# A gated complex recurrence and a mixer on one core: chunks of 128 tokens scaled to their middle in one step, with a checked condition and a branch

## The chip, the cores and the metric

The kernel runs on one core of a Trainium2 chip. The time is device microseconds (us) of one execution on that core; the runs shown are separate executions of the same program. A profile is one more execution, taken by the hardware profiler. In it PE is TensorE's matmul row, PEld its weight loads, DVE is VectorE, ACT is ScalarE, POOL is GpSimd and SP is SyncE, which here only issues DMAs.

## The reference, cut to what matters

Two blocks follow each other. The first is a recurrence over 768 tokens for 4 batches of 8 heads of width 48, with a complex gate per token and channel:

```python
mag = np.sqrt(a_re * a_re + a_im * a_im)
scale = np.minimum(mag, 0.999) / (mag + 1e-06)
a_re_n, a_im_n = (a_re * scale, a_im * scale)
for t in range(S):                       # S_re, S_im: (B, H, 48, 48)
    new_re = ar * S_re - ai * S_im
    new_im = ar * S_im + ai * S_re
    S_re, S_im = (new_re + k[t] v[t]^T, new_im)
    y[t] = q[t] @ S_re
```

The second takes y as x, of shape (4, 768, 384), and is a mixer: u = x + (x^T U V)^T with U of 768x32 and V of 32x768, and then out = u + relu(u @ w_ch1) @ w_ch2, with 1536 hidden channels. All is float32, but for the four mixer weights, which arrive as float64 and are converted on the core.

## The kernel before, in words

**Chunks.** Each batch is cut into 6 chunks of 128 tokens, 24 in all; a chunk has two halves of 64. The recurrence is computed as attention within a half, plus what a 48x48 state per head brings from before. A gate's logarithm (ACT and DVE, `magnitudes_of`, in groups of two chunks) is summed over tokens by a matmul, and exp of the sum is a factor on q and of its inverse on k. A gate's angle is summed in the same manner and gives a cosine and a sine, so that q and k have 2 x 48 real channels, padded to 112 rows (`prep`: `weigh` multiplies q and k by the factors `es`; two products write them with cos and sin into the tile QKC; 16 transposes on PE, in four PSUM tiles, turn them into QK of 112 channels x 8 heads x 128 tokens, copied out by ACT).

**Levels.** A factor over many tokens can leave float32's range, so the kernel before scales q and k only to the middle of blocks of 8 tokens and then grows the blocks step by step. `within` (L583) makes the factors to the middle of 8; `of_blocks` (L612) sums the logarithms over spans of 4, 8, 16, 32, 64 and 128 tokens in one matmul per head against the 64 columns of the tile `total`; ACT's exp of them is E, which SP's DMAs (L598) rearrange into T. In `chain`, per chunk:

- `inner` is called three times (L739): 32 matmuls that each give a 32x32 or 32x16 block of scores in PSUM; DVE then copies the entries of one mask from PSUM into DG (`keep`, L745, a predicated copy).
- `times` and `grow` (L330, five per chunk) multiply the halves of QK by the T of the next larger blocks on DVE.
- four SP DMAs (L777) place the 32x32 diagonal blocks of DG in the score tile AT; `corners` (L789, 16 matmuls) gives the off-diagonal 32x32 blocks of each half, which ACT copies into AT (L794, four copies).
- the grown k is transposed back to tokens x channels (`ks ps`, L810, 8 matmuls, ACT copies at L812).

**State.** dk (L825) is k^T v of each half. `onward` carries the state: GM = G(i-1) x T + dk of half 0, then G(i) = GM x T + dk of half 1, each a multiplication (L330) and an addition (L333) on DVE. The output y of a half is AT^T v (L856) plus q times the state before it (L864), and ACT copies it into xo (L873, four copies).

**Mixer.** `mixer(m)` handles two chunks and can start when a whole batch is through: `rank` (L898) needs all six xo of the batch. `up` (L939) or, from m = 6, the form with fewer products `few` (L997); then `down` (L1085) or `down_two` (L1128). These are PE's large matmuls, 12 mixers in all.

**The order of the work.** Nothing is issued when it is recorded: `Plan` keeps every piece with engine, estimated cost, what it reads and writes and which ring of buffers it takes. `Plan.order` then simulates the five engines and writes out one order for each; among pieces that are ready an engine takes the one with the least urgency, and URGENCY is a table of numbers per kind of work (weights w1 and w2, gates, angles, prep, levels, rest) and chunk or piece. Where PE would have nothing to do before the first "mixing" piece, the plan puts in a filler: a `spare` matmul of the identity (L1252), 203 of them. In PE's order `tr` is the transposes of `prep`. Before the first `rank` of batch 0 PE has only chunk work and fillers; after that, mixers of the batch before run between the chunks of the next; behind the last chunk three mixers are left.

**Buffers.** PSUM tags have two tiles each: T (gates, transposes), A (scores, `ks ps`), Y (dk and y share it), M (mixer). QKC has one tile, VP three, AT and DG two, G two, GM one.

Of the kernel before, what the change touches and what calls it, by code (L numbers as in the profile page):

```python
# [23 lines left out]
BLK = 32  # L24

URGENCY = {
    "w1": {0: -1281.04, 1: -1220.88, 2: -1207.45, 3: 315.61, 4: 369.7, 5: 444.04, 6: 70.95},
    "w2": {0: -1266.56, 2: -21.8, 4: -981.82, 6: -74.99, 8: 354.48, 10: -1170.63, 12: 259.42},
    "gates": {0: 253.11, 1: -1390.93, 2: -0.7, 4: -1280.16, 6: 565.76, 8: -1068.17, 10: -187.84, 12: -54.04, 14: 550.2,
        16: 60.85, 18: -1317.29, 20: 219.78, 22: -1069.82},  # L30
    "angles": {0: -1303.82, 1: -1298.68, 2: -1227.51, 4: 58.46, 6: 57.41, 8: -1315.3, 10: -1053.02, 12: 620.73,
        14: 187.25, 16: -891.55, 18: 148.92, 20: -161.38, 22: -1298.55},
    "prep": {0: -1294.88, 1: 125.6, 2: -26.13, 3: 96.73, 4: 102.92, 5: 146.86, 6: 553.65, 7: 283.9, 8: 120.02,
        9: -991.17, 10: -32.91, 11: 113.94, 12: -202.96, 13: 14.8, 14: 318.58, 15: 357.43, 16: 269.94, 17: 521.08,
        18: 158.53, 19: -163.04, 20: 127.47, 21: 184.1, 22: 205.57, 23: -1204.94},
    "levels": {0: 201.22, 1: 294.56, 2: -15.94, 3: 207.38, 4: -1236.01, 5: 275.3, 6: 572.46, 7: 14.34, 8: -1057.92,
        9: 306.71, 10: 125.53, 11: 133.52, 12: 287.15, 13: 373.35, 14: 82.96, 15: 592.16, 16: 289.79,
        17: -1204.78, 18: -1075.08, 19: 91.86, 20: 733.17, 21: -1309.23, 22: 119.93, 23: -1230.17},
    "rest": {0: 93.55, 1: 47.27, 2: 273.41, 3: 257.67, 4: -1050.04, 5: -1068.08, 6: -1240.77, 7: -1208.87, 8: -1033.73,
        9: -1290.81, 10: 34.85, 11: -1143.56, 12: -162.29, 13: -197.24, 14: -1046.5, 15: 612.4, 16: 244.97,  # L40
        17: -1261.21, 18: 98.64, 19: -1031.75, 20: -1297.46, 21: 239.78, 22: 384.61, 23: 164.23},
}
# [145 lines left out]
@with_exitstack  # L188
def kernel(
    ctx: ExitStack,  # L190
    tc: tile.TileContext,
    q: bass.AP,
    k: bass.AP,
# [9 lines left out]
    out: bass.AP,  # L203
):


# [36 lines left out]
    SIZES = (4, 8, 16, 32, 64, 128)  # L243
    NTOT = CH // 2
    NP = 128 // R
# [8 lines left out]
    def urgency(kind, n):  # L254
        if kind == "load":
            return n - 20
        if kind in ("totals", "place"):
            return n - 100
        if kind in ("small", "mixing"):
            return n + (1000 if kind == "mixing" else -1000)  # L260
        return URGENCY[kind][n]

# [51 lines left out]
    def SP(cost, *a, **kw):  # L314
        plan.add("SP", max(cost, 0.65), *a, late=2.0 if cost > 0.65 else 1.4, **kw)
# [34 lines left out]
    prefix = singles.tile([128, CH], FP, name="prefix")  # L350
    mask = singles.tile([128, 6, BLK], I32, name="mask")
    mid = singles.tile([128, CH], FP, name="mid")
# [38 lines left out]
    AT, DG, VP = [], [], []  # L391
    QKC = singles.tile([128, H, 2, DP], FP, name="QKC")
    nc.gpsimd.memset(QKC, 0.0)
    GATE = singles.tile([128, 6, GC * DM], FP, name="gate")
# [3 lines left out]
    TS = []  # L398
    for n in range(3):
        TS.append(singles.tile([DQ, GC, H * NTOT], FP, name="T%d" % n))  # L400
        nc.gpsimd.memset(TS[n], 1.0)
    for n in range(3):
        VP.append(singles.tile([128, H, D], FP, name="VP%d" % n))
    for n in range(2):
        AT.append(singles.tile([128, H, HC], FP, name="AT%d" % n))
        DG.append(singles.tile([128, H, BLK], FP, name="DG%d" % n))
        nc.gpsimd.memset(AT[n], 0.0)
        nc.gpsimd.memset(DG[n], 0.0)

    def constants():  # L410
        SP(0.4, ("load", 0.1), lambda: nc.sync.dma_start(out=prefix, in_=spans[:, PRE * CH:(PRE + 1) * CH]), writes=[("prefix", 0)])
        SP(0.6, ("load", 1.2), lambda: nc.sync.dma_start(out=mask, in_=masks), writes=[("mask", 0)])

# [118 lines left out]
    def gates(g):  # L532
# [54 lines left out]

        def totals():
            e, tt = ("E", g), ("T", g)
            buffer(e, "E", 1, [128, GC, HH, NTOT])  # L590
            ring(tt, "T", TS)
            lo, hi = GROUPS[g]
            for part in PARTS[g]:
                for i in range(*part):
                    of_blocks(i, ("gates", part[0]))
            for u in range(2):
                for w in range(2):
                    SP(0.65, ("totals", lo), lambda u=u, w=w: nc.sync.dma_start(  # L598
                        out=get(*tt)[u * DP:u * DP + D, 0:hi - lo, w * HH * NTOT:(w + 1) * HH * NTOT],
                        in_=get(*e)[w * 64:w * 64 + D, 0:hi - lo].rearrange("p c h b -> p c (h b)")), [e], [tt + ((u, w),)])  # L600

        def of_blocks(i, R1):
# [80 lines left out]
    def prep(i):  # L683
# [9 lines left out]
        for u in range(2):  # L693
            qkc = ("qkc", 2 * i + u)
            ring(qkc, "qkc", [QKC])
            DVE(c_dve(2 * DM), R1, lambda u=u, qkc=qkc: mul(
# [16 lines left out]
    def chain(i):  # L713
        c = where(i)[1]
        RL, RR = ("levels", i), ("rest", i)
        QK, DGi, ATi, VPi = ("QK", i), ("DG", i), ("AT", i), ("VP", i)
        ring(DGi, "DG", DG)
        ring(ATi, "AT", AT)
# [46 lines left out]

        yield from inner(5, 2)


        times(RL, 4, 16, 8, H * CH - 8, 0)
        yield from inner(1, 8)  # L770
        times(RL, 4, 16, 0, H * CH + 8, 2)
        grow(RL, 8)
        yield from inner(0, 16)
        for j in range(CH // BLK):
            js = slice(j * BLK, (j + 1) * BLK)
            to = slice(j % 2 * BLK, j % 2 * BLK + BLK)
            SP(0.65, ("place", i), lambda js=js, to=to: nc.sync.dma_start(out=get(*ATi)[js, :, to], in_=get(*DGi)[js]), [DGi],  # L777
               [ATi + (("d", js.start),)])
        grow(RR, 16)

        ps1 = ("corners", i)
        psum(ps1, "A", [128, HH, BLK], [128, 4 * HH, BLK])

        def corners():
            for p in range(HH):
                for u in range(2):
                    for r in (0, 64):
                        h, to = 2 * p + u, r + u * BLK
                        nc.tensor.matmul(out=get(*ps1)[to:to + BLK, p], lhsT=k_of(h)[:, r:r + BLK],  # L789
                                         rhs=q_of(h)[:, r + BLK:r + 2 * BLK], start=True, stop=True, tile_position=(0, to))  # L790
        yield 0.38, RR, corners, [QK], ps1, ATi, 8 * HH
        for r in (0, 64):
            for u in range(2):
                ACT(0.32, RR, lambda r=r, u=u: nc.scalar.copy(  # L794
                    out=get(*ATi).rearrange("p (a u) t -> p a u t", u=2)[r:r + BLK, :, u, BLK:2 * BLK],
                    in_=get(*ps1)[r + u * BLK:r + (u + 1) * BLK]), [ps1], [ATi + (("c", r, u),)])
        grow(RR, 32)

        G, mid_G, last = ("G", i), ("GM", i), c == NCH - 1
        ks, dk = ("ks", i), [("dk", (i, r)) for r in range(2)]  # L800
        buffer(ks, "ks", 1, [128, H, DQ])
        buffer(mid_G, "GM", 1, [DQ, H, D])
        rows_k = HC if last else CH
        for hh in range(2):
            ps = ("ks ps", (i, hh))
# [11 lines left out]
        for r in parts_k:  # L817
            psum(dk[r], "Y", [128, H, D], [128, H, DP])

        def state(h0):  # L820
            for h in range(h0, h0 + HH):
                for r in parts_k:
                    at = slice(r * HC, (r + 1) * HC)
                    for x, end in ((0, DP), (DP, DQ)):
                        nc.tensor.matmul(out=get(*dk[r])[x:end, h], lhsT=get(*ks)[at, h, x:end], rhs=get(*VPi)[at, h],  # L825
                                         start=True, stop=True, tile_position=(r * HC, x))
# [5 lines left out]
        def onward(to, of, r):  # L832
# [5 lines left out]
            DVE(c_dve(DM), RR, lambda: add(get(*to), get(*to), get(*dk[r])[0:DQ]), [dk[r]], [to])  # L838
        onward(mid_G, ("G", i - 1) if c else None, 0)
        if not last:  # L840
            onward(G, mid_G, 1)

        y, xi = [("y", (i, r)) for r in range(2)], ("xo", i)
# [343 lines left out]


    constants()
    weights()  # L1190
# [52 lines left out]
    for f in waits:  # L1243
        f()
    chunks(NG - 1)
    spare = []

# [8 lines left out]
    for ins in nc.cur_bb.bb.instructions:  # L1256
        if ins.engine in last:
            tc.add_manual_dep(ins, last[ins.engine], mybir.DependencyInfo(
                mybir.DependencyClass.NoSync, mybir.DependencyReason.DATA), reason="order")
        last[ins.engine] = ins.name  # L1260


# [45 lines left out]
```

## Time and profile before

| | |
|---|---|
| three runs | 696.73, 697.74 (median), 700.15 us |
| profiled execution | span 696.8 us; that is also within 0.1 us of the fastest run, and no other time of it is recorded |
| PE, PEld busy | 673.7 us (97%), 594.2 us (85%) |
| DVE, ACT, POOL busy | 538.9 us (77%), 416.5 us (60%), 51.8 us (7%) |
| granted TensorE clock | 0.997 |
| DMA | 53.24 MB, 165203 packets, of which 154016 are under 512 B |
| dearest DVE group | L330 on QK: 120 instructions, 145.4 us |
| fillers | 203 in the program, 406 records, 57.8 us |

A float32 matmul stands in the trace as two records, a transpose as one. A few records can be missing. Busy time of a group is the union of its records, and their ends are modelled, so the busy times of PE's groups add up to more than PE's. The start-to-start distance of two pieces in the timeline says what a piece costs in the stream. "issue" is time in which an engine waited for nothing that the profile shows.

### The profile page before, as it was taken

What the parts mean: (1) busy time and instruction counts of PE and PEld (TensorE: products, weight loads), DVE (VectorE), ACT (ScalarE), POOL (GpSimd) and SP (SyncE); (2) the same over time, 40 slices, a digit from 0 to 9 for tenths busy, and PEclk for the clock granted to TensorE, in tenths of its full rate; (3) what the DMA queues carried; (4) which work ended last, traced back from release to release, by engine and by line L of the source; (5) the groups of instructions that cost most, each with busy time, mean ns of one, the idle gap of its engine ahead of it and who ended that gap; (6) DMA issues with size and microseconds to landing.
All of it is one profiled execution on the core that took longest, in us unless ns stands there. A gap on an engine that the chain in (4) does not pass through costs nothing.

```text
span 696.8 us, 26972 instructions
## 1 busy us (share of the span) xinstructions
PE 673.7 (97%) x12116; PEld 594.2 (85%) x12116; DVE 538.9 (77%) x877; ACT 416.5 (60%) x776; POOL 51.8 (7%) x92
## 2 busy tenths in 40 slices
PE   8988998999999999999999999999998999999998
PEld 8777777786787888888888888889998898999998
DVE  5899999888998887758598668779886884555734
ACT  7879874968886897958796745434524325031230
POOL 5100000012100010001010100000000000000000
PEclk9999999999999999999999999999999999999999
DMA  8884745699514442432243031222111010000000
GB/s 202 190 187 86 172 99 105 171 222 189 110 36 97 87 92 54 94 70 57 51 89 78 3 86 40 45 43 56 37 36 18 14 41 2 18 7 24 7 18 24
DMA packets 165203, 53.24 MB, mean 76 GB/s; under 512 B 154016, under 2 KB 160352, under 8 KB 165088
## 3 DMA queue, kind: packets, MB, share of 16 engines
q1 hardware_dynamic: 161008, 42.26, 28.0%
q0 software_dynamic: 4080, 9.27, 5.9%
q8 instruction: 95, 1.56, 0.9%
q14 instruction: 20, 0.16, 0.1%
HBM read 33.59 MB, written 4.72 MB: 55 GB/s over the span
## 4 chain that ended last, share of the span: by engine, by line
PE 75%; ACT 10%; DVE 9%; issue 3%; DMA 2%; SPq 0%; DVEq 0%; ACTq 0%
PE down L1128 20%; PE few L997 12%; PE up L939 10%; PE tr L705 6%; PE inner L739 5%; ACT gate L327 4%; PE y L864 3%; PE dk L825 3%; DVE QK L330 2%; PE ks ps L810 2%; PE ph L650 2%; PE es ps L583 2%; PE tot L612 2%; PE y L856 2%; PE spare L1252 1%
## 5 line engine op out<-in xcount | busy, mean ns | idle before, releaser
L330 DVE TENSOR_TENSOR QK<-QK,T 112x1024 f32<-112x1024 f32 x120 | 145.4, 1217 | 7.6 <-PE corners L789 4.0
L939 PE MATMUL up<-uT,w 128*128 128x256 f32 x432 | 98.9, 382 | 0.0
L939 PEld LDWEIGHTS up<-uT,w 128*128 128x128 f32 x432 | 80.5, 190 | 12.3
L1005 ACT COPY h<-few 128x512 f32<-128x512 f32 x36 | 20.6, 586 | 95.0 <-PE few L997 78.2
L708 ACT COPY QK<-tr 112x512 f32<-112x512 f32 x96 | 53.0, 586 | 36.5 <-PE tr L705 36.1
L1128 PE MATMUL down<-w,h 128*128 128x192 f32 x396 | 74.1, 331 | 0.0
L327 ACT ACTIVATE gate<-gate 128x768 f32<-128x768 f32 (+1 forms) x91 | 70.2, 789 | 5.3 <-DMA gate<-in_a_re_dram 2.2
L1128 PEld LDWEIGHTS down<-w,h 128*128 128x128 f32 x396 | 63.7, 190 | 3.2 <-issue 1.1
L739 PEld LDWEIGHTS inner<-QK 112*32 112x32 f32 x4608 | 45.4, 109 | 20.7 <-issue 15.4
L333 DVE TENSOR_TENSOR h<-few,h 128x512 f32<-128x512 f32 x54 | 37.1, 690 | 31.3 <-PE few L997 28.7
L739 PE MATMUL inner<-QK 112*32 112x16 f32 (+1 forms) x4608 | 51.3, 190 | 10.4 <-issue 9.3
L1252 PE MATMUL spare<-ident 128*128 128x128 f32 x406 | 57.8, 289 | 1.7 <-POOL ident masks.py:199 1.5
L330 DVE TENSOR_TENSOR QKC<-qk,cs 128x768 f32<-128x768 f32 x48 | 45.7, 953 | 14.9 <-PE tr L705 13.4
L705 PE MATMUL tr<-ident,QKC 128*112 128x128 f32 x384 | 54.2, 276 | 2.8 <-ACT QK L708 1.1
L1252 PEld LDWEIGHTS spare<-ident 128*128 128x128 f32 x406 | 52.0, 200 | 5.5 <-POOL ident masks.py:199 1.5
L333 DVE TENSOR_TENSOR xo<-down,xo 128x192 f32<-128x192 f32 (+1 forms) x79 | 29.6, 385 | 28.5 <-PE down L1128 28.3
L705 PEld LDWEIGHTS tr<-ident,QKC 128*112 128x112 f32 x384 | 42.1, 133 | 10.9 <-ACT QK L708 3.0
L997 PE MATMUL few<-gate,w 128*128 128x128 f32 x336 | 44.0, 279 | 0.0
L1072 POOL DMA_DIRECT2D out_dram<-xo x32 | 18.8, 586 | 321.0 <-DVE xo L333 289.2
L873 ACT COPY xo<-y 64x192 f32<-64x192 f32 x96 | 30.0, 313 | 18.8 <-PE y L864 17.4
L997 PEld LDWEIGHTS few<-gate,w 128*128 128x128 f32 x336 | 40.6, 194 | 0.5
L1128 PE MATMUL down<-stage 128*128 128x192 f32 x198 | 36.8, 329 | 0.1
(131 smaller groups left out, 1242.6 us busy)
## 6 DMA issues: line engine op xcount, KB each, us to landing
stage<-in_moe_w_ch_dram SPq DMA_DIRECT2D x12, 768.0 KB, 5.8
gate<-in_a_re_dram SPq DMA_DIRECT2D x24, 192.0 KB, 3.5
gate<-in_a_im_dram SPq DMA_DIRECT2D x24, 192.0 KB, 3.7
qk<-in_q_dram SPq DMA_DIRECT2D x24, 192.0 KB, 3.4
qk<-in_k_dram SPq DMA_DIRECT2D x24, 192.0 KB, 4.2
VP<-in_v_dram SPq DMA_DIRECT2D x24, 192.0 KB, 3.4
T<-E SPq DMA_DIRECT2D x48, 96.0 KB, 2.7
w<-stage POOLq DMA_DIRECT2D x12, 384.0 KB, 6.0
```

The lines of the kernel that those rows point to most:

```text
L327: return nc.scalar.activation(out=o, in_=i, func=f, **kw)
L330: nc.vector.tensor_tensor(out=o, in0=a, in1=b, op=OP.mult)
L333: nc.vector.tensor_tensor(out=o, in0=a, in1=b, op=OP.add)
L705: nc.tensor.transpose(out=get(*ps)[0:DQ, j], in_=get(*qkc)[:, hh * HH + j].rearrange("p u d -> p (u d)")[:, 0:DQ], identity=ident)
L708: ACT(c_act(HH * CH) - 0.05, R1, lambda u=u, hh=hh, ps=ps: nc.scalar.copy(out=get(*QK)[:, u, hh * HH:(hh + 1) * HH], in_=get(*ps)[0:DQ]), ...
L739: nc.tensor.matmul(out=get(*ps)[js, h], lhsT=k_of(h)[:, js], rhs=part(q_of(h)[:, js], "p"), start=True, stop=True, tile_position=(0, j * BLK))
L825: nc.tensor.matmul(out=get(*dk[r])[x:end, h], lhsT=get(*ks)[at, h, x:end], rhs=get(*VPi)[at, h], start=True, stop=True, tile_position=(r * ...
L873: ACT(c_act(HH * D), RR, lambda r=r, u=u: nc.scalar.copy(out=get(*xi).rearrange("p (a u d) -> p a u d", u=2, d=D)[r * HC:(r + 1) * HC, :, ...
L939: nc.tensor.matmul(out=get(*ps)[:, e], lhsT=w1[:, f, (ff + e) * 128:(ff + e + 1) * 128], rhs=get(*uT)[:, f], start=(f == 0), stop=(f == KD ...
L997: nc.tensor.matmul(out=get(*ps)[:, q], lhsT=w()[:, q * 128:(q + 1) * 128], rhs=v[0](), start=(n == 0 and q == 0), stop=True, skip_group_ch ...
L1128: nc.tensor.matmul(out=get(*to)[:, part], lhsT=x(j), rhs=y[:, j], start=(first and j == 0), stop=(j == KH - 1), skip_group_check=not first)
L1252: nc.tensor.matmul(out=spare[0], lhsT=ident, rhs=ident, start=True, stop=True)
```

## The change

The function `tile_gateloop...` becomes `body(..., general, worst, ...)`. With `general` false, `body` is the new program; with `general` true it is the program before, with plain urgencies (`n` in place of the table). The new entry records the new program, reads one word from SBUF into a register of every engine, and has the general program behind a branch:

```diff
+def tile_gateloop__then__mixer_low_rank_kernel(tc: tile.TileContext, *args):
+    with tc.tile_pool(name="worst", bufs=1) as pool:
+        worst = pool.tile([1, 1], I32, name="worst")
+        body(tc, False, worst, *args)
+        found = tc.nc.values_load(worst, ...)
+        with tc.If(found != 0):
+            body(tc, True, worst, *args)
```

In the new program the factors reach to the middle of the whole chunk in one step (`mid` is the sum to token 63 less the sum to the token; `total` has two columns, the sums over the two halves):

```diff
+            def middle():
+                nc.gpsimd.tensor_tensor(out=mid, in0=half.to_broadcast([128, CH]), in1=prefix, op=OP.subtract)
+                nc.gpsimd.tensor_copy(out=total[:, 0:1], in_=half)
+                nc.gpsimd.tensor_tensor(out=total[:, 1:2], in0=prefix[:, CH - 1:CH], in1=half, op=OP.subtract)
...
+        def of_halves(i, R1):
+            def sums():
+                for h in range(H):
+                    for u in range(2):
+                        nc.tensor.matmul(out=get(*ps)[u * 64:(u + 1) * 64, h], lhsT=get(*l)[:, at + h * D:at + h * D + 64],
+                                         rhs=total, start=True, stop=True, tile_position=(0, u * 64))
+            table(0.25, R1, lambda: act(falls[:, i], get(*ps)[0:DQ], AF.Exp, scale=-1.0), [ps], [("falls", i)])
```

`of_halves` has 16 matmuls per chunk where `of_blocks` had 8, with 2 moving columns where there were 64. E, T and the DMAs between them are gone. `inner`, `times`, `grow`, the placing DMAs, `corners` with its copies and `ks ps` with its copies are left out; in their place:

```diff
+        def whole():
+            psum(ps, "A", [128, H, HC])
+            def products():
+                for h in range(H):
+                    for r in range(2):
+                        at = slice(r * HC, (r + 1) * HC)
+                        nc.tensor.matmul(out=get(*ps)[at, h], lhsT=k_of(h)[:, at], rhs=q_of(h)[:, at], start=True, stop=True,
+                                         tile_position=(0, r * HC))
+            DVE(c_dve(H * HC), RL, lambda: nc.vector.copy_predicated(
+                out=get(*ATi), mask=mask.unsqueeze(1).to_broadcast([128, H, HC]), data=get(*ps)), [ps, ("mask", 0)], [ATi])
...
+        yield from (levels() if general else whole())
...
+        ks, dk = ("ks", i) if general else ("qkc", 2 * i + 1), [("dk", (i, r)) for r in range(2)]
```

So a chunk has 16 matmuls of 112 rows x 64 columns against 64 moving columns, and one predicated copy of 512 columns. dk reads k straight from QKC, which is now one tile for q and a ring of three for k. The state takes one multiplication and two additions per chunk in place of two and two:

```diff
+        def through(to, of, r):
+            DVE(c_dve(DM), RR, lambda: add(get(*to), get(*dk[r])[0:DQ], get(*of)), [dk[r], of], [to])
+
+        if c and not general:
+            B = ("G", i - 1)
+            DVE(0.16, RR, lambda: mul(between[:, i], falls[:, i - 1, :, 1], falls[:, i, :, 0]), ...)
+            DVE(c_dve(DM), RR, lambda: mul(get(*B), get(*B), between[:, i].unsqueeze(2).to_broadcast([DQ, H, D])), ...)
```

After the last chunk's piece is recorded, `verdict` finds the smallest of all `falls` (a DVE reduction of 112 x 384, one transpose on PE, a second reduction) and writes 1 into `worst` if it is below exp(-30). With the inputs of the reference a half's sum of logarithms lies between -7.3 and -5.3, so the word is 0.

The URGENCY table is replaced by another one throughout:

```diff
 URGENCY = {
-    "w1": {0: -1281.04, 1: -1220.88, 2: -1207.45, 3: 315.61, 4: 369.7, 5: 444.04, 6: 70.95},
+    "w1": {0: 30.69, 1: -1312.12, 2: -1.77, 3: 1300.77, 4: 396.41, 5: 683.84, 6: -1360.01},
...
```

The mixer's code is the same. The program up to the branch has 4037 instructions on PE for 6384, 710 on DVE for 879, 633 on ACT for 778, 145 on SP for 289, and 160 fillers for 203 (counts of the built programs, one per instruction).

## The prediction

> **What bounds the kernel now.** I read the page's head first, then the chain of work that ended last (section 4).
>
> ```profile
> span 696.8 us, 26972 instructions
> ...
> PE 673.7 (97%) x12116; PEld 594.2 (85%) x12116; DVE 538.9 (77%) x877; ACT 416.5 (60%) x776; POOL 51.8 (7%) x92
> ...
> PE 75%; ACT 10%; DVE 9%; issue 3%; DMA 2%; SPq 0%; DVEq 0%; ACTq 0%
> ```
>
> PE is never idle for long, and the chain runs mostly through PE. But an average hides stages, and part of PE's time is filler. So I cut the span where each batch's `rank` starts on PE (133.2, 301.6, 454.7 and 590.4 us by the timeline) and asked for the engines' busy time in each stretch; columns are PE, PEld, DVE, ACT, POOL, then clock, DMA share, GB/s.
>
> ```profile
> 0.00:133.20 133.20, 120.27 (x2759) 103.58 (x2760) 118.56 (x181) 102.62 (x196) 16.29 (x39) 1.00 0.69 152
> 133.20:301.60 168.40, 165.84 (x2927) 136.29 (x2928) 142.55 (x207) 138.21 (x240) 15.52 (x20) 1.00 0.52 111
> 301.60:454.70 153.10, 151.96 (x2839) 130.85 (x2839) 115.25 (x179) 101.70 (x187) 10.14 (x15) 1.00 0.26 56
> 454.70:590.40 135.70, 132.62 (x2843) 124.14 (x2846) 104.83 (x186) 51.39 (x117) 4.97 (x9) 0.99 0.14 30
> 590.40:696.80 106.40, 103.05 (x763) 99.38 (x762) 57.74 (x127) 22.54 (x38) 4.88 (x9) 1.00 0.05 16
> ```
>
> In the first stage 192 of the 203 fillers run (order of the program): 384 records at about 0.135 us (eight in 1.09 us by the chain), 52 us of PE's 120.3. The real bound there is DVE, 118.6 of 133.2 and idle mainly in the first 30 us, with ACT next at 102.6. In the other four stages PE is full with real work (98%, 99%, 98%, 97%): there only PE time counts, and what DVE and ACT save is worth nothing.
>
> **What PE loses and gains.** The groups' busy times overlap at their edges, so I price pieces by start-to-start distance in the timeline (first column the start).
>
> ```profile
> 256.75 1.32 PE L739 MATMUL inner<-QK 112*32 112x32 f32 x128
> 258.00 1.56 PE L583 MATMUL es ps<-GL,mid 128*128 128x384 f32 x4
> ...
> 264.52 1.15 PE L612 MATMUL tot<-total,GL 128*64 128x64 f32 x32
> 265.61 2.86 PE L939 MATMUL up<-uT,w 128*128 128x256 f32 x12
> ...
> 271.63 1.29 PE L739 MATMUL inner<-QK 112*32 112x16 f32 x128
> 272.85 5.45 PE L939 MATMUL up<-uT,w 128*128 128x256 f32 x24
> ...
> 279.10 0.76 PE L789 MATMUL corners<-QK 112*32 112x32 f32 x64
> 279.80 1.24 PE L1128 MATMUL down<-w,h 128*128 128x192 f32 x6
> ```
>
> 128 `inner` records take 1.25 us, 64 `corners` records 0.70, 32 `tot` records 1.09 (34 ns each). `ks ps` takes 0.77 to 0.86 us per chunk (575.27 to 576.04 and 535.54 to 536.40). Then:
>
> - `inner` out: 4608/128 x 1.25 = -45.0; `corners` out: 768/64 x 0.70 = -8.4; `ks ps` out: 24 x 0.81 = -19.4.
> - Waits of PE in front of these pieces that nothing explains:
>
> ```profile
> PE inner L739 <- issue: 9.3, 9, 2.3
> ...
> PE corners L789 <- issue: 1.2, 1, 1.2
> ```
>
>   They go with them: -10.5. No other piece has so many short records in a row.
> - Scores in: 24 x 32 = 768 records of 112x64 weights, 64 moving columns. Nearest rows: `tot` (128x64, 64 columns) 34 ns and `y<-G,QK` (112x64, 48 columns; 16 records from 255.69 to 256.19) 31 ns. I take 34: +26.1.
> - `tot`: 768 records for 384, with 2 moving columns. Does a narrow product cost less? `inner` with 16 columns takes 1.22 us and with 32 takes 1.25, and 48 and 64 columns cost 31 and 34: the pace follows the weights' columns, not the moving ones. So I take 34 ns again: +13.1. The other end is the cheapest product of the trace, 9.8 ns: 768 x 9.8 - 13.1 = -5.6.
>
> Real PE work: -45.0 - 8.4 - 19.4 - 10.5 + 26.1 + 13.1 = **-44.1 us**. Fillers: 43 fewer x 0.27 = **-11.7**. They come out only if the first stage really gets shorter, so this is checked next.
>
> **The first stage.** DVE loses per chunk five `times` (145.4/120 = 1.21) and three copies into DG (0.44 + 2 x 0.29), and 10 state multiplications of 0.55 become 5: 36.3 + 6.1 + 2.8 = 45.2 for six chunks. It gains six predicated copies of 512 columns; the rows of 128 and 256 columns take 291 and 439 ns, so 0.74 each by the line through them: +4.4, and five `between` at 0.2 (nearest row 128x32, 190 ns): +1. DVE: 118.6 - 39.8 = 78.8. ACT loses 24 corner copies (0.256) and 12 `ks` copies (0.533), and E of 256 columns becomes 16: 6.1 + 6.4 + about 1.2. ACT: 88.9. So ACT is late next. PE in the new order up to `rank`: real work 120.3 - 52.0 - 11.3 (inner) - 2.1 - 4.9 + 4.4 (tot) + 6.5 (scores) = 60.9, with 151 fillers x 0.27 = 40.8, together 101.7; of the 12.9 us of idle time 6.4 stood in front of `inner` and `corners` (5.2 + 1.2), 6.5 stay: **108**. ACT would then be 82% busy, 77% now. I believe it, but not firmly: angles and gates alternate between ACT, DVE and PE, and ACT's own idle time now is 30 us. If that stays whole, the stage ends at 119, and the fillers only turn into idle time.
>
> **Hidden edits.** The 96 placing DMAs and 48 of E to T leave SP; no wait of PE's list is on a DMA outside the first microseconds, so this is worth nothing by itself. What depended on T (`times`, the state) depends on ACT's `falls` directly, a shorter path. The copy into AT follows the scores at once and its 0.74 us lie beside mixer matmuls. `verdict` is two reductions near 0.55 us (the 384-column rows) and two tiny operations on DVE in the third stage, where DVE has 38 us idle, and one transpose of 0.1 us on PE. k's QKC is held until dk has read it; with three tiles, two prepared chunks ahead are not held up. The three more memsets of QKC (0.95 us each) replace T's three on POOL. The mixer sits unchanged; 30 of its `down` products (168 to 138) stand before the last `rank` now instead of behind it, a move within PE's stream.
>
> **What becomes late.** The carry of the state: dk, two additions and a multiplication, y, four ACT copies of 0.31, and dk of the next chunk needs the two PSUM tiles that y held. Before, `ks ps` and `few` pieces filled these places. In the new order the last four chunks stand close together with 1 us of `down` between steps whose additions take 0.2 + 2 x 0.55, or whose copies take 4 x 0.31 + 0.3: some 0.5 us open at half a dozen places. I add **+4**.
>
> **The end.** All five engines load the word into a register and jump twice: into the empty side, where semaphores are brought to the general program's counts, and out. `worst` is ready long before. Below, this is free: the last DVE addition ends at 694.2 and the span at 696.8, and the last output DMA is in flight meanwhile. Above: 2.0 us for the load (the landing of the smallest DMA, 1.5 KB) and two jumps at 2.3 (the longest unexplained wait of PE): 6.6. I take **+3**, between, because SP issues the last DMA and only then loads and jumps.
>
> Here the Trainium skill speaks against the change: "Runtime: NRT & Kernel Launch", section Instruction fetch mechanics, holds that a taken branch out of the prefetched window stalls until the page is fetched, and that kernels do better unrolled; it gives no length. No branch with a far target is in this trace. "Advanced Engine Details and Errata", section Control Flow Timing, gives about 108 ns for a compare-and-branch, an estimate of +0.2 for both jumps, and the sum would be 3 us lower. [...]
>
> **The sum.** 696.8 - 44.1 - 11.7 + 4 + 3 = 648.0 of the profile's span. The median of the runs is 0.9 above that span, so **649**.
>
> **Rivals.**
>
> 1. *The first stage is held by ACT and the last chunks wait on each other.* For it: ACT is 77% busy there and feeds every other engine; 12 copies per chunk remain. Against: DVE, on which ACT waits, gets 40 us freer. Price: the stage ends at 119 (+11), and the carry costs 1.5 us more at six places (+9): **669**.
> 2. *Narrow products are cheap*, 9.8 ns for `tot` (-18.7): **630**. Against: the equal pace of 16 and 32 columns.
> 3. *Slower: the carry of the state is bare.* One cycle is dk 1.1, additions 1.3, y 1.6, copies 1.5, handovers of some 0.2 each, near 6 us, of which PE works 2.7. If 3.3 us stood open for each of 24 chunks, +79 in place of +4: **723**. It decides from 52.8/24 = 2.2 us per chunk. Against: in the second to fourth stages the order has mixer pieces between nearly all these steps. For: in the first stage there are none but fillers.
> 4. *It does not do what it says:* the word is not 0 and the general program follows, about twice the time, near 1350. By the inputs' sums (at least -7.3 against -30) this can hardly be.
> 5. *The end costs tens of us*, five engines fetching from two places: near **695**, no change. Nothing in the trace shows such a price.
>
> **Chances.** The forecast (640 to 660) 0.62; rival 1 (to 676) 0.18; rival 2 (630 to 640) 0.12; rival 5 0.03; rival 3 0.04; rival 4 0.01. A measurement tells 0.5% (3.5 us) from no change. Faster: 0.62 + 0.18 + 0.12 = 0.92; same 0.03; slower 0.05. The range takes the forecast, rival 2 and rival 1: 630 to 674.
>
> **What would show it.** First `rank` near 108 us with 14 us fewer fillers in front (119 for rival 1); `score` and `tot` records at 34 ns start to start; no "issue" row of 9 us left for PE; DVE near 375 us, ACT near 363; PE idle between batches still a few us; some 3 us more between the last addition and the span's end. Wrong it would be if PE showed tens of us of waits on G, GM or xo, if ACT's idle time in the first stage stayed at 30 us, or if the span held a long gap at the end.

## The result and the profile after

The changed kernel takes **629.43 us** (median of four runs, 627.97 to 632.85) where the kernel before takes 697.24 beside it (692.64 to 700.15): a ratio of 0.904 with an interval of 0.899 to 0.908. The forecast was 649, the range 630 to 674. The direction was right, the gain is 68 us in place of 48, and the time lies 0.6 us under the range's lower bound of 630, by less than the runs differ among themselves.

The head of the page after, the engines' busy times and the chain of work by engine:

```profile
span 628.2 us, 17308 instructions
...
PE 611.7 (97%) x7615; PEld 544.7 (87%) x7615; DVE 396.5 (63%) x709; ACT 361.5 (58%) x632; POOL 48.4 (8%) x78
...
PE 84%; ACT 10%; DVE 4%; issue 1%; DMA 1%; SPq 0%; ACTq 0%
```

PE is still 97% busy and carries more of the chain (84% for 75%), "issue" has gone from 3% to 1%, and DVE from 9% to 4%. Cut again where each batch's `rank` starts (103.8, 257.1, 393.1 and 528.0 us), with the columns of the table before:

```profile
0.00:103.80 103.80, 95.81 (x1606) 82.88 (x1606) 85.36 (x142) 87.29 (x159) 15.24 (x27) 1.00 0.83 181
103.80:257.10 153.30, 153.05 (x1930) 126.80 (x1927) 103.09 (x159) 121.03 (x202) 11.85 (x16) 1.00 0.45 96
257.10:393.10 136.00, 135.78 (x1776) 119.70 (x1775) 82.71 (x142) 89.13 (x151) 10.74 (x16) 0.99 0.24 52
393.10:528.00 134.90, 133.45 (x1616) 125.54 (x1614) 73.78 (x153) 42.29 (x84) 6.26 (x11) 1.00 0.07 19
528.00:628.20 100.20, 93.61 (x703) 89.81 (x702) 51.59 (x114) 21.75 (x37) 4.32 (x8) 0.99 0.05 17
```

The stages took 133.2, 168.4, 153.1, 135.7 and 106.4 us and take 103.8, 153.3, 136.0, 134.9 and 100.2. The first gives 29 us, the second and third 32, the other two 7. ACT is now the busiest engine of the first stage after PE, 84% of it. In the second and third, PE is idle for 0.25 and 0.22 us in all: PE hardly waits there, and these stages are as long as PE's stream in them.

The groups that are new or changed (busy time, mean ns of one record, idle time ahead), and the only unexplained wait that PE has left:

```profile
L854 PE MATMUL score<-QK 112*64 112x64 f32 x768 | 25.8, 223 | 1.1 <-issue 1.1
L639 PE MATMUL tot<-total,GL 128*64 128x2 f32 x768 | 24.3, 198 | 0.0
L857 DVE COPY_PREDICATED AT<-mask,score 128x512 f32<-128x512 int32 x24 | 17.3, 732 | 15.5 <-PE score L854 15.4
```

```profile
PE score L854 <- issue: 1.1, 1, 1.1
```

The mean of 223 ns is a latency: on average the next record starts 32 ns later. Priced by start-to-start distance, as in the prediction, PE's stream compares so (us; each row sums the distances of its records to the next record in the trace; "after" less "before"):

| term | forecast | measured |
|---|---|---|
| `inner` out | -45.0 | -47.8 |
| `corners` out | -8.4 | -9.2 |
| `ks ps` out | -19.4 | -19.0 |
| scores in | +26.1 | +24.3 (31.6 ns a record) |
| `tot` doubled | +13.1 | +9.7 (30.4 ns for 35.3) |
| all other pieces | 0 | -6.6 |
| fillers | -11.7 | -13.4 |
| PE idle (issue -10.5, new waits +4) | -6.5 | -9.8 |
| end, load and jumps | +3 | +3.3 |
| sum | -48.8 | -68.5 |

The spans differ by 68.6. No single row holds the 20 us that were missed; seven of the nine lean the same way. The experiments ask what these have in common.

### The profile page after: what moved, and what is told of

It is laid out like the page before. It is cut to its first block, busy times and chain, and to the rows that moved or that the text cites. A ratio compares the mean times of both kernels' runs of the same rounds, so it can differ in the third digit from the quotient of the medians.

```text
span 628.2 us, 17308 instructions
## 1 busy us (share of the span) xinstructions
PE 611.7 (97%) x7615; PEld 544.7 (87%) x7615; DVE 396.5 (63%) x709; ACT 361.5 (58%) x632; POOL 48.4 (8%) x78
## 4 chain that ended last, share of the span: by engine, by line
PE 84%; ACT 10%; DVE 4%; issue 1%; DMA 1%; SPq 0%; ACTq 0%
PE down L1211 22%; PE up L1022 15%; PE few L1080 13%; PE tr L750 5%; ACT gate L333 4%; PE tot L639 4%; PE score L854 4%; PE dk L894 3%; PE y L947 3%; PE es ps L608 3%; PE down L1168 3%; PE ph L692 2%; PE y L939 2%; PE mixed L997 2%; ACT cs L333 2%; ACT QK L753 1%
## 5 line engine op out<-in xcount | busy, mean ns | idle before, releaser
L1211 PE MATMUL down<-w,h 128*128 128x192 f32 x396 | 72.4, 329 | 0.0
L336 DVE TENSOR_TENSOR QKC<-qk,cs 128x768 f32<-128x768 f32 x48 | 44.3, 954 | 13.0 <-ACT cs L333 8.0
L1352 PE MATMUL spare<-ident 128*128 128x128 f32 x320 | 43.3, 287 | 1.4 <-POOL ident masks.py:199 1.4
L1352 PEld LDWEIGHTS spare<-ident 128*128 128x128 f32 x320 | 40.2, 201 | 3.6 <-POOL ident masks.py:199 1.4
L333 ACT ACTIVATE h<-h 128x512 f32<-128x512 f32 x36 | 22.7, 630 | 30.4 <-DVE h L339 30.4
L333 ACT ACTIVATE h<-up 128x512 f32<-128x512 f32 x36 | 21.3, 593 | 30.4 <-PE up L1022 30.4
L1211 PEld LDWEIGHTS down<-stage 128*128 128x128 f32 x198 | 32.6, 190 | 1.2
```

Of the source, the lines that this page charges most:

```text
L333: return nc.scalar.activation(out=o, in_=i, func=f, **kw)
L336: nc.vector.tensor_tensor(out=o, in0=a, in1=b, op=OP.mult)
L1211: nc.tensor.matmul(out=get(*to)[:, part], lhsT=x(j), rhs=y[:, j], start=(first and j == 0), stop=(j == KH - 1), skip_group_check=not first)
L1352: nc.tensor.matmul(out=spare[0], lhsT=ident, rhs=ident, start=True, stop=True)
```

## The experiments

Theory A, from the prediction: the new program shortens PE's stream, and the order is worth only its fillers. Rival B: the new urgencies are worth much more than that. Three smaller questions go with them: whether fillers matter at all, whether DVE's time matters, and what the end costs. The ratios are against the kernel before, timed beside each kernel in three groups, in which it took 697.04, 700.09 and 698.85 us; so a difference in us between kernels of different groups can be off by some 3 us. "Lost clock" is the sum of (1 - granted clock) over stretches of 1 us in the profiled execution: 1.7 us in the profiles of before and after, so their difference owes nothing to it.

**The changed kernel again**, as the standard of its group.

> The changed kernel unaltered, as the measure for the other three of this group: 628 to 631 us, span near 628.

630.26 us (627.72 to 632.93), ratio 0.904 [0.899, 0.909]; span 626.3. The result repeats.

**Without the register load and the branch**, and so without the general program behind it.

```diff
-        found = tc.nc.values_load(worst, ...)
-        with tc.If(found != 0):
-            body(tc, True, worst, *args)
```

> Leaves out the register load, the branch and the general program; the new program and the verdict stay as they are. In the changed kernel's profile the last addition ends 5.9 us before the span does, 2.6 us in the kernel before. If the load and the two jumps cost the 3.3 us between them: 625 to 627 us, span near 625, and 2.6 us after the last addition. Rival: the 3.3 us are the output's landing or chance, and the end is free: 628 to 630.

627.37 us (624.74 to 631.5), ratio 0.898 [0.894, 0.902]. The intervals overlap with the kernel's above, so the ratio alone does not tell them apart. The end of the trace does. These are the last additions into xo by the timelines (start, us, engine, line, operation), first of the changed kernel (span 628.2), then without the branch (span 629.7):

```profile
621.98 0.36 DVE L339 TENSOR_TENSOR xo<-down,xo 128x192 f32<-128x192 f32 x1 [1.39 <-PE down L1211]
```

```profile
626.84 0.36 DVE L339 TENSOR_TENSOR xo<-down,xo 128x192 f32<-128x192 f32 x1 [1.39 <-PE down L1211]
```

From the end of that addition to the end of the span it is 5.9 us with the branch, 2.5 without and 2.6 in the kernel before: load and jumps cost **3.3 us**, the +3 of the prediction. (This profiled execution lost 6.8 us of clock and is one of the longer ones; the runs with a granted clock of 1.00 took 624.74 and 624.84.)

**Without fillers**, the order of all else the same.

```diff
-        (plan.ops[n][4] if n >= 0 else idle)()
+        (plan.ops[n][4] if n >= 0 else idle if general else int)()
```

> The same order, but none of the 160 identity products that fill PE. If they only stand where PE would wait anyway, the first rank still starts at 104 us plus or minus 2 and the time is 627 to 632; the 41 us of fillers turn into idle time of PE in the first stage. Rival A: they hold up real pieces behind them, first rank near 95 and 620. Rival B: without them PE's granted clock falls in the first stage, real pieces there take longer, first rank at 108 or later and 634 or more.

640.12 us (634.63 to 640.7), ratio 0.915 [0.909, 0.920]: 10 us slower than the changed kernel beside it. Its first stage by the windows:

```profile
0.00:115.80 115.80, 80.94 (x1306) 62.24 (x1308) 86.20 (x142) 88.16 (x159) 15.35 (x27) 0.79 0.74 162
```

All of the loss is here, 115.8 us for 103.8, at a granted clock of 0.79; the other stages take 153.6, 134.3, 135.0 and 100.1 us, as in the changed kernel. The real pieces there get slower (the transposes take 19 us of the stream for 12) and what depends on them waits. So the fillers pay for themselves: without them PE's idle stretches cost clock. That the first stage has 43 fewer of them is no saving by itself; they go because the stage is shorter.

**The new program with the old urgencies.**

```diff
-    "w1": {0: 30.69, 1: -1312.12, 2: -1.77, 3: 1300.77, ...
+    "w1": {0: -1281.04, 1: -1220.88, 2: -1207.45, 3: 315.61, ...
```

> The new program with the urgencies of the kernel before. Theory (what left PE's stream is the gain, the order only keeps PE fed): 632 to 642 us. Rival (the new urgencies gave much of the gain, above all the 20 us beyond the forecast): 645 or more, with PE waits between the batches. Neither expects less than 626.

656.49 us (654.87 to 659.01), ratio 0.939 [0.937, 0.942]. The expectation of theory A fails and rival B holds: with this program, some 25 of the 68 us belong to the table. By the spans (696.8, 653.1, 628.2) the program alone gives -43.7, where the prediction had -37.1 without the fillers (-44.1 + 4 + 3), and the new table gives **-24.9**, where the prediction had -11.7. The stages of this kernel are 116.0, 145.4, 154.4, 121.4 and 115.9 us, so the old table leaves the first one 12 us longer. Of the 24.9, 11.4 are fillers (195 for 160), 2.7 are PE's idle time, and up to 5.1 are lost clock (6.8 for 1.7). This is the stretch of its first stage where that happens:

```profile
44.00:48.00 4.00, 3.96 (x124) 3.29 (x126) 3.97 (x7) 1.64 (x4) 0.85 (x1) 1.00 1.07 183
48.00:52.00 4.00, 3.71 (x48) 3.40 (x46) 2.76 (x7) 2.31 (x3) 0.00 (x0) 0.57 0.84 221
52.00:56.00 4.00, 4.00 (x70) 3.60 (x69) 3.90 (x6) 1.55 (x4) 0.00 (x0) 0.50 1.04 200
56.00:60.00 4.00, 4.00 (x14) 2.69 (x14) 0.28 (x2) 1.11 (x3) 0.85 (x1) 0.65 0.94 204
```

From 48 us on PE is busy for 11.7 of 12 us, yet the clock is near half for some ten microseconds, and DVE and ACT are idle for 5 and 7 of the 12 us. What brings the half clock there is not shown. That leaves some 5.7 us in which the same pieces are simply cheaper in the new order. What differs is the neighbours: counted in the traces, PE goes from one shape of tile to another (128x128, 128x64, 64x64, ...) 283 times in the kernel before, 215 times here and 176 times in the changed kernel. What such a change costs is measured below.

**The old program with the new urgencies**, so that the table is seen by itself.

```diff
 URGENCY = {
-    "w1": {0: -1281.04, 1: -1220.88, 2: -1207.45, 3: 315.61, ...
+    "w1": {0: 30.69, 1: -1312.12, 2: -1.77, 3: 1300.77, ...
```

> The kernel before with the new urgencies. Theory: nothing leaves PE's stream, so no gain, 695 to 715 us, as the table was made for other pieces. Rival (the order itself is better): 685 or less.

735.39 us (734.18 to 739.06), ratio 1.052 [1.047, 1.056], more than was expected. PE's idle time is 33.1 us for 18.6, there are 260 fillers for 203, 296 changes of shape for 283, and the first `rank` comes at 163.0 us. So the table is no better order in itself: it fits the new program only, and gain and loss are an interaction. A table tuned for one program cannot be priced from another's trace.

**Products of the full shape among the scores.** Two kernels with the same work: three products of the identity per chunk into the scores' PSUM tile, which the scores then overwrite, once all ahead of the scores, once each between two heads.

```diff
             def products():
+                for x in (2, 4, 6):
+                    nc.tensor.matmul(out=get(*ps)[:, x:x + 2], lhsT=ident, rhs=ident, start=True, stop=True)
                 for h in range(H):
```

```diff
                 for h in range(H):
+                    if h in (2, 4, 6):
+                        x = h
+                        nc.tensor.matmul(out=get(*ps)[:, x:x + 2], lhsT=ident, rhs=ident, start=True, stop=True)
```

> Three products of the identity (128x128, all of the array) per chunk are put in front of the chunk's first score, into PSUM that the scores overwrite; the order is otherwise as it was. 72 products at 0.225 us are 16 us in PE's stream. Theory: 643 to 649. Rival (PE has room): under 636. This run is the measure for the next one.

> The same three products per chunk, but one each in front of heads 2, 4 and 6: the same work, and 72 more changes from two tiles to the full array and back. Theory (a change costs PE about 0.07 us each way, which would explain why many unchanged pieces became cheaper in the changed kernel): 8 to 12 us above the run with the products in front, 652 to 660. Rival (changes are free, the cheaper pieces have another cause): within 2 us of it.

Ahead of the scores: 652.93 us (652.36 to 654.18), ratio 0.934 [0.932, 0.936], some 23 us more than the changed kernel, above what was expected. Nearly all of the span's +24.2 is the products (19.7, 137 ns a record) and lost clock (5.1, as 6.8 for 1.7). Between the heads: 674.1 us (669.96 to 678.6), ratio 0.965 [0.959, 0.971], 21 us more again, about twice what was expected. Lost clock (6.8 us) and PE's idle time (7.7 and 7.2 us) are the same in both, so neither explains the difference. Two chunks in PE's timeline, first with the products ahead, then between the heads:

```profile
306.69 0.94 PE L852 MATMUL score<-ident 128*128 128x128 f32 x6
307.55 1.15 PE L856 MATMUL score<-QK 112*64 112x64 f32 x32
308.63 0.94 PE L852 MATMUL score<-ident 128*128 128x128 f32 x6
309.50 1.15 PE L856 MATMUL score<-QK 112*64 112x64 f32 x32
310.48 0.62 PE L949 MATMUL y<-GM,QK 112*64 112x48 f32 x16
```

```profile
317.12 0.42 PE L857 MATMUL score<-QK 112*64 112x64 f32 x8
317.47 0.49 PE L854 MATMUL score<-ident 128*128 128x128 f32 x2
317.89 0.45 PE L857 MATMUL score<-QK 112*64 112x64 f32 x8
...
322.40 0.62 PE L950 MATMUL y<-GM,QK 112*64 112x48 f32 x16
```

Nothing waits in either. Apart, 64 score records and 12 products take 3.79 us (306.69 to the next piece at 310.48), mixed 5.28 (317.12 to 322.40). Over the whole span it is 19.4 us for 116 more changes of shape (320 for 204): **0.17 us each**. With that, the 39 changes between old and new table are worth 6.5 us, where 5.7 were left to explain. A rival is that a product pays for writing where the scores write too. The trace speaks against it: the first record of a full-shape product starts 152 ns after the record before it, whether that was a score or a `y`, which shares no tile with it, and the first score behind the products starts 205 ns after the last of them, whether it overwrites a product's columns (between the heads) or not (ahead).

The price is not one of this pair alone. Fitted over all borders between pieces, outside waits and half clock, in the traces of the kernel before, of the old table and of the changed kernel, a border with a change costs 0.16 to 0.17 us more than one without. And of the 107 changes that went from before to after, half of each put down to the piece before it and half to the piece behind, 68.5 went with `inner`, `corners` and `ks ps`, 12 with fillers and 6.5 from `tot`, the scores brought 10 and the verdict's transpose one, and pieces that nobody touched lost 31: 5.3 of the 6.6 us that these became cheaper.

**Scores in quarters.** Four products of 32 weight columns per head in place of two of 64, to see whether the pace goes by the weights' columns.

```diff
-                    for r in range(2):
-                        at = slice(r * HC, (r + 1) * HC)
-                        nc.tensor.matmul(out=get(*ps)[at, h], lhsT=k_of(h)[:, at], rhs=q_of(h)[:, at], ...
+                    for j in range(CH // BLK):
+                        at, of = slice(j * BLK, (j + 1) * BLK), slice(j // 2 * HC, j // 2 * HC + HC)
+                        nc.tensor.matmul(out=get(*ps)[at, h], lhsT=k_of(h)[:, at], rhs=q_of(h)[:, of], ...
```

> The scores in 32 columns of weights on four tiles (32 products per chunk for 16, 64 moving columns each), same result. The pace of the old 32-column products was 9.8 ns a record, so 1536 records x 9.8 = 15 us for the 24.3 us that the scores take now; with 64 moving columns four tiles may not go under about 14 ns: 21 us. If the stream of PE is what counts and dense short records bring no waits: 3 to 9 us less, 620 to 626. Rival: short records in a row bring back the unexplained waits of PE that stood before the old 32-column products (9.3 us): 629 to 635, with an issue row of several us on the scores.

641.3 us (639.65 to 650.68), ratio 0.918 [0.913, 0.922]: 11 us slower, no gain. In the trace the scores are 1536 records at 15.8 ns, 24.2 us, against 768 at 31.6, 24.3 us. With 64 moving columns the pace does go by the weights' columns, so halves cost as much as quarters. Inside a piece, where no border adds to it, it is 14.2 ns a record for the quarters and 29.2 for the halves; `inner` before, also with 32 weight columns but 16 or 32 moving ones, ran at 8.6 and 8.9, so at 32 weight columns the moving ones do count, and the 9.8 of the expectation did not carry over; its bound of about 14 came out. New are unexplained waits, of the pieces that follow:

```profile
PE tr L750 <- issue: 3.0, 1, 3.0
PE tot L639 <- issue: 1.6, 2, 1.0
...
PE dk L894 <- issue: 1.3, 1, 1.3
```

PE's idle time is 13.9 us for 8.8. Such waits stood in front of `inner` before, and they come back when short records are dense again; what causes them is not shown. The profiled execution is the longest of the six (650.68 us), with 17 us of lost clock; four of the others have a granted clock of 0.987 or 0.988. By an estimate from these figures, 5 us of waits and some 6 of clock make up the 11.

**k transposed back** from its finished channels, as before, in place of reading QKC.

```diff
-        ks, dk = ("ks", i) if general else ("qkc", 2 * i + 1), [("dk", (i, r)) for r in range(2)]
+        ks, dk = ("ks", i), [("dk", (i, r)) for r in range(2)]
-        for hh in range(2 if general else 0):
+        for hh in range(2):
```

> One part of the change undone: k for the state comes again from QK through 8 transposes per chunk and ACT copies, in place of being read from QKC. Theory (PE's stream is the bound): 192 transposes at 0.1 us are 19 us, and 48 more pieces between others make PE change its tiling more often; ACT gets 24 us more, mostly beside PE: 648 to 658 us. Rival (they hide in gaps of PE): under 640.

658.54 us (655.42 to 660.57), ratio 0.942 [0.938, 0.946]; 28 us more, just above what was expected. The span grows by 27.3: 19.8 are `ks ps` itself, 5.7 more fillers. The lost clock is 1.7 as in the changed kernel. This term of the prediction (-19.4) was right to half a microsecond, and it shows that one edit moves more than its own time: the first stage grew by 11 us.

**Idle DVE work in the first stage.** 29 multiplications of a 112x1024 tile that nothing reads, some 33 us, behind pieces of the chunks of batch 0.

```diff
+    def extra(i):
+        if not general and i < NCH:
+            mul(load, load, load)
```

> The changed kernel with 29 idle multiplications of 112x1024 on DVE (1.13 us each, on a scratch tile nobody reads), behind pieces of the six chunks of batch 0: 33 us more for DVE in the first stage, the order as it was. If DVE was the bound of the first stage and its relief is what shortened it, the first rank moves from 104 to 118 us or later and the time to 642 or more, about +15 to +25. Rival (ACT holds the stage now): first rank at 104 to 110, +0 to +6.

660.89 us (658.95 to 662.47), ratio 0.944 [0.941, 0.946]. The first stage:

```profile
0.00:133.10 133.10, 110.39 (x1604) 95.57 (x1604) 116.76 (x170) 89.00 (x159) 16.22 (x28) 0.87 0.64 140
```

133.1 us, +29.3 for 31.4 more of DVE, at a granted clock of 0.87; the rest of the span gives the other 3. Time added to DVE lengthens this stage nearly one to one, which fits the bound that the prediction named. Some 17 of the 29 us are lost clock ((1 - 0.87) x 133), so the delay comes in part through PE's clock.

**The same behind the later chunks** (`i >= NCH`): 87 multiplications, 94 us more DVE time.

> The same multiplications behind pieces of the 18 chunks of batches 1 to 3: 87 of them, 98 us more for DVE after the first stage. If PE's stream alone bounds these stages, DVE's relief there is worth nothing and the time stays at 628 to 636. Rival (DVE's relief pays in all stages, which would explain part of the 20 us beyond the forecast): 645 or more, with PE waits on G, GM and AT.

677.76 us (676.38 to 678.05), ratio 0.968 [0.966, 0.971]: some 47 us more than the changed kernel. PE's waits in it:

```profile
PE tr L757 <- DVE QKC L336: 4.6, 6, 1.0
PE y L946 <- DVE AT L864: 4.5, 2, 3.9
...
PE y L946 <- DVE G L339: 4.1, 4, 1.7
```

The second stage takes 177.1 us for 153.3. PE's idle time is 37.7 us for 8.8 and the lost clock 15.3 for 1.7; together 42.5 of the span's 47.6. So DVE time that is added after the first stage does cost in this order; what taking it away gives was not tested.

**Behind the mixers instead.** 88 of them, after additions into xo in the mixers 1 to 8, off the chain from chunk to chunk.

```diff
+                    if not general and 1 <= m <= 8:
+                        for _ in range(0 if y is None else 1 if also is not None else 2):
+                            mul(load, load, load)
```

> As many idle multiplications on DVE in the same stages as in the run that put 87 behind the chunks' pieces (there +48 us), but 88 of them behind the mixers' additions into xo. If it is the distance between the steps of a chunk's chain that costs, and not DVE's total: 631 to 645. If DVE's total work in these stages counts, wherever it stands: 665 or more.

694.42 us (692.3 to 697.52), ratio 0.993 [0.991, 0.996]: 65 us more than the changed kernel for 101 us of DVE time, worse than behind the chunks. That only the chunks' chain feels DVE falls too. PE waits for the additions themselves (`down`, 12.6 us in seven waits, the longest 2.7) and for pieces queued behind them. What one wait does is seen in a small stretch:

```profile
335.72 1.14 PE L1213 MATMUL down<-stage,more 128*128 128x192 f32 x6
339.85 0.65 PE L752 MATMUL tr<-ident,QKC 128*112 128x128 f32 x4 [2.99 <-DVE QKC L336]
340.33 3.31 PE L1213 MATMUL down<-stage 128*128 128x192 f32 x12
343.43 1.57 PE L752 MATMUL tr<-ident,QKC 128*112 128x128 f32 x8
```

```profile
338.00:341.00 3.00, 1.15 (x9) 1.16 (x10) 3.00 (x5) 0.69 (x2) 0.00 (x0) 1.00 0.00 0
341.00:344.40 3.40, 3.40 (x14) 3.30 (x14) 3.37 (x5) 0.86 (x2) 0.78 (x1) 0.51 0.60 116
```

After a wait of 2.99 us the granted clock is 0.51 for 3.4 us: twelve `down` records take 3.31 us, which take 2.12 in the changed kernel, and eight `tr` take 1.57 for 1.04. The half clock adds 1.7 us to the wait. Nine of the ten such stretches of this kernel stand right behind a wait of 2.0 to 3.1 us; one further wait of 2.05 us has none behind it. Idle time +44.2 and lost clock +17.0 (18.7 for 1.7) make 61 of its 67.5 us.

## Why the prediction was right, and where it was not

**What bounds the kernel** was read rightly: PE's stream in four stages, DVE in the first. Every removed piece came out within 3 us of its price. The reason was right and the sum too small: it missed 20 us. That the range reached down to 630 is owed to rival 2, whose reason did not come, and that is luck.

**The step that failed** is this one: "Fillers: 43 fewer x 0.27 = -11.7", as the whole value of the new order. It measured -24.9 in the trace with the old table beside it: 11.4 of fillers as forecast, and 13.5 that no step priced (idle time 2.7, lost clock 5.1, cheaper pieces 5.7, which 39 fewer changes of tile shape at 0.17 us account for within a microsecond). The diff showed that the table was replaced, and the order of both programs could be laid side by side beforehand; I counted the fillers in it and not the neighbours.

**The program by itself** was 6.6 us better than its sum of -37.1. `inner` and `corners` gave 3.6 more (a piece also takes its changes of shape with it), `scores` and `tot` cost 1.8 and 3.4 less than at 34 ns. That price was a whole piece's, its borders included. Inside a piece, `tot` runs at 29.2 ns a record with 2 moving columns as it did with 64, and the scores at 29.2 too; the averages of 30.4 and 35.3 ns differ by the borders. So the prediction read rightly that the moving columns do not count at 64 weight columns. Rival 2 (9.8 ns) gave the right time for a wrong reason.

**The first stage** was forecast at 108 and came at 103.8; rival 1's 119 did not come. With the old table it would have been 116.0, so the stage was in the end a question of order. ACT was priced well there (88.9, measured 87.3), DVE badly (78.8, measured 85.4). In total DVE is 396.5 us for "near 375". One reason is visible: DVE's groups sum to 588 us in the profile of before, and DVE is busy for 539, since the records of neighbours overlap; 120 `times` at their mean of 1.21 us take away less than 145 us of busy time.

**What becomes late** (+4) did not come: in the second and third stages PE is idle for 0.25 and 0.22 us. Rival 3, the slower one, needed 2.2 us open per chunk; PE's whole idle time is 8.8 us.

**The unexplained waits** went from 10.5 to 1.1 us with the short records, as said, and the quarters brought 5.9 back; their cause stays open. **The end** cost 3.3 for +3. Rivals 4 and 5 did not come.

**"What DVE and ACT save is worth nothing"** in the later stages is not borne out as a general sentence. Added to the new kernel, each microsecond of DVE there costs 0.5 to 0.67. PE's order is fixed in the program, what is late holds up what stands behind it (PE's idle time is 37.7 and 53.0 us there for 8.8), and waits of 2 to 3 us were mostly followed by half clock. Adding is not the mirror of taking away: how much of the new table's gain is open to it only because DVE has 142 us less to do stays open. It is likely, since the same table loses 35 us on the old program, but there more than DVE's time differs.

No kernel tried here beats the changed one by more than can be told; the one without the branch comes closest and lacks the guard.

## What to carry to other kernels

Price a full in-order engine by start-to-start distances, piece by piece; that came out within 3.4 us a term here. Price the borders between pieces apart from the pieces: a price taken from a whole piece holds its borders too. Then price the order as a term of its own: count in both programs how often PE changes the shape of its tile and where it waits for two microseconds or more, and do not take a new table of priorities for a by-product of the edit it came with. An idle share on another engine need not be slack: here PE took DVE's results in a fixed order, and time added to DVE cost at least half of itself wherever it was added.

## What the runs showed of the hardware

- A change of tile shape between products on PE cost 0.17 us (19.4 us for 116 in the pair of kernels; 0.16 to 0.17 in a fit over three other traces). The Trainium skill's "TensorEngine Tiling (Array Packing)", Tiling Modes, Key Properties, says that changing the mode drains TensorE, without a length; the pair of kernels fits this and gives one.
- Half clock came in portions of 3.4 us, each worth 1.7 us. In the kernel with DVE work behind the mixers, nine of ten stretches stood right behind waits of 2.0 to 3.1 us. The skill's "TensorE: Matmul & The Clock Gate", Part 1: The HAM clock gate, gives an idle window of about 3.4 us as the condition, running free of the kernel. The portion's length agrees; the waits here were shorter than the window, and some portions began where PE had not stood at all for 7 us, one at 296 us of the changed kernel among them. What brings those stays open.
- The changed kernel's time went with the granted clock: 627.72 us at 0.999, 632.93 at 0.987.
- Start to start inside a piece, float32 records with 64 weight columns came every 29.2 ns with 2, 48 and 64 moving columns alike; with 32 weight columns (112 rows) every 8.6, 8.9 and 14.2 ns with 16, 32 and 64 moving columns.
- Loading a word into a register of all engines and jumping over a long program cost 3.3 us once.
